# The first pair of blocks of a convolution and SwiGLU kernel: tokens ahead of weights, idle TensorE products, pieces in a new order

## The chip, the cores and the metric

The kernel runs on one core of a Trainium2 chip. The metric is the device time of one execution in microseconds; the time of a kernel is the median of its runs.

A core has five engines that run side by side, each through its own queue in order: TensorE (PE in the profile, its weight loads PEld) multiplies matrices, VectorE (DVE) and ScalarE (ACT) do elementwise work, GpSimd (POOL) does elementwise work more slowly, and SyncE (SP) issues transfers. An engine that waits holds up all that stands behind it in its queue. SBUF is the memory on the core, PSUM holds TensorE's results in 8 banks.

## The reference

32768 tokens of 192 numbers go through a short causal convolution and a SwiGLU network without bias. All inputs and outputs are float32 to the kernel.

```python
# attention block: x (8, 4096, 192), weight (8 heads, 7 taps)
w = softmax(weight)                                  # over the 7 taps of a head
out[b, s, h, g] = sum_k w[h, k] * x_pad[b, s + k, h, g]   # 24 channels share a head's taps
# network: x (32768, 192), w_gate and w_val (192, 1536), w_out (1536, 192)
rms = np.sqrt(np.mean(x * x, axis=-1, keepdims=True) + 1e-06)
xn = x / rms * rms_g
g = xn @ w_gate
silu = g * (1.0 / (1.0 + np.exp(-g)))
val = xn @ w_val
return (silu * val @ w_out).astype(np.float32)
```

The matrices arrive as 64-bit floats, as two 32-bit words each, and the kernel takes them apart itself.

## The kernel before

The tokens are cut into 32 pairs of blocks; a pair is 1024 tokens, in two blocks g of 512. The hidden width of 1536 is 12 chunks of 128, taken as 4 units u of 3 chunks f. In every product the two halves of TensorE's rows work side by side: the lower 64 rows compute the gate, the upper 64 the value. The product of a pair has these parts:

- conv (L327): 7 taps; ScalarE multiplies tokens by a tap into a tile m (L356, eight instructions per tap, one per head), VectorE adds (L360). The first tap, and the first three of the first pair, are done on VectorE alone (L341, L346). At its end it loads the tokens of the next pair (load, L143), for which there is one buffer.
- norm (L364): squares on ScalarE (L371), the factor by GpSimd's power (L377, L380), scaling on ScalarE and VectorE (L389, L384).
- place (L459), fetch (L484), x_sums (L496): VectorE transposes blocks of 32 (L471), SyncE writes them to a scratch in DRAM (L476) and reads them back as xb, channels on the partitions (L491); VectorE forms 11 sums of blocks in xc (L501).
- unit (L530): for the pairs after the first, the products of a unit are a fast scheme that needs 15 products (L568) in place of 18, with copies and sums on the other engines. Its order is written out in PLAN. It takes 11 working tiles from the list tiles and gives them back.
- outer (L654): the product with the output matrix (L661), 96 steps on each half, whose results are added up (L681, L685) and stored (L690). A block's first pass takes chunks 0 to 8 for all four groups of 128 tokens, then 9 to 11.

The first pair is different, since nothing is ready. Its tokens come by load(0), followed in SyncE's queue by the weights of unit 0 (load_in), two parts of the output matrix (load_out) and unit 1. After the convolution, cross (L403) scales and transposes through TensorE: the factor r is a power on GpSimd (L426), diag holds eight diagonal matrices of the factors (L430, L435), 24 products of y with them (L441) give the transpose in PSUM, and 12 copies bring it to xb (L456, L454). The first pair's products are the plain ones (L608): 24 groups of 6 matmuls (L621), each followed by a SiLU (L631) and a product (L638), which gives back a PSUM bank.

All weights are converted in this first pair. convert (L233) takes exponent and mantissa of each number apart on VectorE (L241, L245, L248), scales them on ScalarE (L252, L253, and L256 for the output matrix), and puts them together on VectorE (L258, L268, L273) or GpSimd (L264, L265). A unit's input weights are converted at once, 128x1152 numbers an instruction. The output matrix comes in six parts of 128x384 through two buffers of the pool outs; the next load is issued by GpSimd when a part is converted. w_sums (L295) forms on GpSimd the sums of weights that the fast scheme needs, 19 instructions a unit; it overwrites parts of the plain weights, and so waits for the plain products of that unit.

The order of the first pair on all engines is written by hand: the string START names one piece of work a letter (x cross, i input weights, o and O output matrix, c convolution of pair 1, n its norm, t its transposes, p products, s SiLUs, v values, w sums of weights). From the output stage on, pieces are put at places in a queue, in units of 1/100 of the time that a product of 512 columns takes; base is the start of the output stage.

Of the kernel before, what the change touches and what calls it, by code (L numbers as in the profile page):

```python
# [11 lines left out]
F32 = mybir.dt.float32  # L12
AF = mybir.ActivationFunctionType
# [6 lines left out]
def kernel(  # L20
# [166 lines left out]
    def words(w):  # L187
        return w.bitcast(U32).rearrange("r (n two) -> r n two", two=2)

    def load_in(u, q):  # L190
        cols = slice(u * NF * P, (u + 1) * NF * P)
        t = big.tile([P, 2, NF, T], F32, name="ht")
        t = t[:].rearrange("p a f t -> p (a f t)")[:, 0 : KP * NF * P * 2].bitcast(U32)
        t = raw["in", u] = t.rearrange("p (k n two) -> p k n two", k=KP, two=2)
        for w, rows in ((moe_w_gate, LOW), (moe_w_val, UPP)):
            for k in range(KP):
                q.dma_start(out=t[rows, k], in_=words(w)[k * HP : (k + 1) * HP, cols, :])

    def load_out(i, q=nc.gpsimd):
        if i >= NO:  # L200
            return
        t = outs.tile([P, T // P, D], F32, name="o_sb")
        t = t[:].rearrange("p j d -> p (j d)").bitcast(U32)
        t = raw["out", i] = t.rearrange("p (f d two) -> p f d two", f=PF, two=2)
        for f in range(PF):
            r = (i * PF + f) * P
            q.dma_start(out=t[:, f], in_=words(moe_w_out)[r : r + P, :, :])

    load_in(0, nc.sync)
    load_out(0, nc.sync)  # L210
    load_out(1, nc.sync)
# [100 lines left out]
    def convert_in(u):  # L312
        if u >= NU:
            return
        dst = wf[u][:, 0:9, :].rearrange("p (k f) n -> p k (f n)", k=KP)
        yield from convert(raw.pop(("in", u)), exp_i, mf_i, dst, rg_sb)

    def convert_out(i):
        dst = wo_sb[:, i * PF : (i + 1) * PF, :]
        yield from convert(raw.pop(("out", i)), *cvt[i % 2], dst)  # L320
        load_out(i + 2)
# [5 lines left out]
    def conv(p, alone=0):  # L327
# [6 lines left out]
        for k in range(K):  # L334
# [19 lines left out]
            for h in range(H):  # L354
                hs = slice(h * GS, (h + 1) * GS)
                nc.scalar.mul(m[:, :, hs], xk[:, :, hs], taps[:, h, k : k + 1])  # L356
                if h % 2:
                    yield
            if k > 0:
                nc.vector.tensor_tensor(out=y[:], in0=y[:], in1=m[:], op=ALU.add)  # L360
            yield
# [40 lines left out]

    def cross():  # L403
        y = ys.pop(0)
        ss = work.tile([P, NJ], F32, name="ss")
        sq = work.tile([P, D], F32, name="sq")
        na = NJ // 2
        for j in range(na):
            nc.scalar.activation(
                out=sq[:], in_=y[:, j, :], func=AF.Square, accum_out=ss[:, j : j + 1]  # L410
            )
            yield
        nc.scalar.copy(out=ends[:, :, 0:HP], in_=y[:, :, 2 * HP :])
        yield
        s2 = prods.tile([P, NJ, D], F32, name="m")
        nc.vector.tensor_tensor(
            out=s2[:, na:, :], in0=y[:, na:, :], in1=y[:, na:, :], op=ALU.mult
        )
        nc.vector.tensor_reduce(out=ss[:, na:], in_=s2[:, na:, :], axis=AX.X, op=ALU.add)
        nc.vector.tensor_copy(out=ends[:, :, HP:], in_=y[:, :, 0:HP])  # L420
        yield
        r = work.tile([P, NJ], F32, name="r")
        nc.vector.tensor_scalar(
            out=r[:], in0=ss[:], scalar1=1.0 / D, scalar2=1e-6, op0=ALU.mult, op1=ALU.add
        )
        nc.gpsimd.tensor_tensor(out=r[:], in0=r[:], in1=nhalf[:], op=ALU.pow)  # L426
        yield
        for j in range(NJ):
            if j % 2:
                nc.vector.tensor_scalar(  # L430
                    out=diag[:, j, :], in0=unity, scalar1=r[:, j : j + 1],
                    scalar2=None, op0=ALU.mult,
                )
            else:
                nc.scalar.mul(diag[:, j, :], unity, r[:, j : j + 1])  # L435
            yield
        nq = T // P
        for j in range(NJ):
            for k in range(KP):
                two = ends[:, j, :] if k == 2 else y[:, j, k * HP : (k + 2) * HP]  # L440
                nc.tensor.matmul(  # L441
                    out=ps[k * 2 + j // nq][:, (j % nq) * P : (j % nq + 1) * P],
                    lhsT=two, rhs=diag[:, j, :], start=True, stop=True, skip_group_check=True,
                )
            yield
            if j % nq == nq - 1:
                for k in range(KP):
                    src = ps[k * 2 + j // nq][:].rearrange("p (j g q) -> p g q j", j=nq, g=2)
                    for h in range(2):
                        dst = xb[HALF[h], :, (k + h) % KP, :]  # L450
                        dst = dst.rearrange("p g (q j) -> p g q j", j=NJ)
                        dst = dst[:, :, :, j - nq + 1 : j + 1]
                        if h and j == NJ - 1:
                            nc.vector.tensor_copy(out=dst, in_=src[HALF[h]])  # L454
                        else:
                            nc.scalar.copy(out=dst, in_=src[HALF[h]])  # L456
                        yield

# [45 lines left out]
    ps = [psum.tile([P, T], F32, name=f"ps{i}") for i in range(8)]  # L504
    HALF = (LOW, UPP)
# [3 lines left out]
    tiles = [work.tile([P, T], F32, name=f"tile{i}") for i in range(11)]  # L509
# [98 lines left out]
    def plain(hts):  # L608


        groups = [(u, g, f) for u in range(NU) for g in (1, 0) for f in range(NF)]
        held = {}
# [119 lines left out]
    def done(it):  # L732
        for _ in it:
            pass
# [5 lines left out]

    START = (
        "xxxxxxxixxxxxxxxxoxixcxcxxxixxxxxixxxxxxxxciccicpccccpsivOpsiccvpciscicpscvcvcpi"
        "scovpwcsivpcwsOvpiswccvpiscciwcpscvwvcicpsvipwoOcspsvviwpsviwpsiwpsvcwpsvvopOswo"
        "cOpvwosOnvpnnnpossvnoOpvOopnnOnnststtstttvvv"
    )
    done(conv(0, 3))
    load_in(2, nc.sync)
    load_in(3, nc.sync)
    hts = []
    p, sl, v = plain(hts)  # L750
    pieces = {
        "x": cross(),
        "i": itertools.chain(*[convert_in(u) for u in range(NU)]),
        "o": itertools.chain(*[convert_out(i) for i in range(0, NO, 2)]),
        "O": itertools.chain(*[convert_out(i) for i in range(1, NO, 2)]),
        "c": conv(1, 1), "n": norm(1, share=True), "t": place(1),
        "p": p, "s": sl, "v": v,
        "w": itertools.chain(*[w_sums(u) for u in range(NU)]),
    }
    for i in START.replace(" ", ""):  # L760
        next(pieces[i], None)
    for i in "iocntpsvO":
        done(pieces[i])
    ws = pieces["w"]
# [10 lines left out]
    WLATE = (160, 439, 719, 999, 1279, 1558, 1838, 2118)  # L775
    ROOM = (465, 526)
    for p in range(PAIRS):
# [14 lines left out]
        put(base + LAG, functools.partial(fetch, p + 1))  # L792
        if p == 0:
            later(ws, *[base + i for i in WLATE])
# [5 lines left out]
        later(x_sums(p + 1), *[base + i for i in (1690, 2020, 2060)],  # L800
              *[base + 2345 + 70 * i for i in range(len(XSUM) - 2)])
# [30 lines left out]
```

## Time and profile before

| | us |
|---|---|
| median of 3 runs | 2740.15 (2739.7 to 2740.2) |
| the profiled execution | 2740.65 |
| its span, first to last instruction | 2738.8 |
| TensorE busy | 2689.3 (98%) |
| VectorE busy | 2282.8 (83%) |
| ScalarE busy | 2208.5 (81%) |
| GpSimd busy | 1239.9 (45%) |

The profile is of one execution. Busy time is the time in which an engine worked on an instruction, including a matmul that runs at a lowered clock. Lines such as L621 are lines of the kernel before. The time of the execution includes 1.85 us around the span. A matmul of float32 appears as two records for each instruction.

| the first pair in the timeline | start, us |
|---|---|
| first work on tokens (L341, L356) | 11.8 |
| last addition of the convolution (L360) ends | 26.45 |
| first transposing product (L441) | 31.6 |
| first plain product (L621) | 43.09 |
| first output product (L661) | 114.8 |
| first product of the second pair (L568) | 152.5 |

### The profile page before, as it was taken

Reading aid. Unit: us, or ns where it says so; the run is one execution under the profiler, and the core shown is the slowest. Engines: PE = TensorE matmul, PEld = TensorE weight load, DVE = VectorE, ACT = ScalarE, POOL = GpSimd, SP = SyncE. Lnnn points to the kernel's source line nnn. Section 1 sums busy time; section 2 is a strip of 40 time slices with the busy share of each in tenths; the row PEclk is TensorE's granted clock in tenths of the full one; section 3 lists DMA queues with packets and bytes.
Section 4 is the critical chain, followed back from the end, with each engine's and each line's share of the span. In section 5 each row is a group of like instructions: output and inputs, shape, how many; then the busy total and the mean of one; then the engine's idle time right before and its main releaser. Section 6 shows DMA issues by size and latency. Waiting matters only on the chain.

```text
span 2738.8 us, 54219 instructions
## 1 busy us (share of the span) xinstructions
PE 2689.3 (98%) x20192; PEld 2049.6 (75%) x20192; DVE 2282.8 (83%) x3642; ACT 2208.5 (81%) x5011; POOL 1239.9 (45%) x1034
## 2 busy tenths in 40 slices
PE   4899999999999999999999999999999999999999
PEld 2568888778887788887788876677766777766777
DVE  7788889888888888888888898888888888988854
ACT  7588888888888888888888888888887888888854
POOL 2854344544345533445434445434455343454433
PEclk9999999999999999999999999999999999999999
DMA  4212222112221122221121221112211222211110
GB/s 121 79 44 68 56 68 60 43 44 58 66 62 47 49 57 56 67 61 42 44 67 56 67 52 50 45 56 68 62 41 50 61 56 67 62 41 44 44 39 13
DMA packets 93945, 152.90 MB, mean 56 GB/s; under 512 B 6769, under 2 KB 63857, under 8 KB 89593
## 3 DMA queue, kind: packets, MB, share of 16 engines
q1 hardware_dynamic: 92608, 147.84, 20.8%
q8 instruction: 158, 2.59, 0.4%
q0 software_dynamic: 512, 1.57, 0.2%
q14 instruction: 107, 0.87, 0.1%
q10 hardware_dynamic: 560, 0.03, 0.0%
HBM read 99.87 MB, written 49.55 MB: 55 GB/s over the span
## 4 chain that ended last, share of the span: by engine, by line
PE 98%; DVE 1%; DMA 0%; POOL 0%; issue 0%; ACT 0%; SPq 0%; DVEq 0%; POOLq 0%
PE ps L568 58%; PE ps L661 37%; PE ps L621 2%; DMA x_sb<-in_x_dram 0%; DVE y L360 0%; PE ps L672 0%; DVE y L346 0%; PE ps L441 0%; ACT xb L456 0%; DMA o_sb<-in_moe_w_out_dram 0%; DVE nt L471 0%; DVE y L384 0%; DVE xc L258 0%; POOL r L426 0%; DVE y L341 0%
## 5 line engine op out<-in xcount | busy, mean ns | idle before, releaser
L568 PE MATMUL ps<-xc,wf 64*128 64x512 f32 x4960 | 1521.8, 593 | 0.0
L568 PEld LDWEIGHTS ps<-xc,wf 64*128 64x128 f32 x4960 | 764.7, 187 | 396.3 <-issue 177.2
L661 PE MATMUL ps<-wo_sb,ht 64*128 64x192 f32 x12288 | 1052.5, 323 | 3.6 <-DVE ht L638 3.6
L661 PEld LDWEIGHTS ps<-wo_sb,ht 64*128 64x128 f32 x12288 | 1048.8, 187 | 3.9 <-DVE ht L638 3.9
L568 PE MATMUL ps<-xb,wf 64*128 64x512 f32 x2480 | 1019.6, 589 | 0.0
L597 POOL TENSOR_TENSOR ht<-ht,tile 128x512 f32<-128x512 f32 x620 | 773.4, 1272 | 535.1 <-ACT tile L594 534.5
L577 ACT ACTIVATE tile<-ps 128x512 f32<-128x512 f32 x1488 | 821.1, 598 | 166.3 <-PE ps L568 141.8
L568 PEld LDWEIGHTS ps<-xb,wf 64*128 64x128 f32 x2480 | 434.6, 187 | 210.9 <-issue 105.5
L356 ACT ACTIVATE m<-x_sb,taps 128x192 f32<-128x192 f32 x1520 | 543.2, 444 | 8.5 <-DMA x_sb<-in_x_dram 5.9
L585 POOL TENSOR_TENSOR tile<-tile,tile 128x512 f32<-128x512 f32 x248 | 315.2, 1271 | 221.6 <-DVE tile L581 211.7
L590 DVE TENSOR_TENSOR tile<-ps,tile 128x512 f32<-128x512 f32 x620 | 411.7, 681 | 0.4 <-PE ps L568 0.4
L360 DVE TENSOR_TENSOR y<-y,m 128x1536 f32<-128x1536 f32 x190 | 335.5, 1766 | 86.0 <-ACT m L356 79.6
L590 DVE TENSOR_TENSOR ht<-ps,tile 128x512 f32<-128x512 f32 x620 | 400.4, 678 | 0.0
L594 ACT ACTIVATE tile<-tile 128x512 f32<-128x512 f32 x620 | 379.0, 624 | 22.5 <-DVE tile L590 20.9
L377 POOL TENSOR_SCALAR r<-ss 128x8 f32<-128x8 f32 x31 | 27.6, 891 | 643.3 <-ACT sq L371 643.2
L590 DVE TENSOR_TENSOR ps<-ps,tile 128x512 f32<-128x512 f32 x248 | 173.4, 699 | 132.7 <-PE ps L568 130.6
L577 ACT ACTIVATE ps<-ps 128x512 f32<-128x512 f32 x372 | 216.3, 581 | 45.4 <-PE ps L568 34.5
L685 DVE TENSOR_TENSOR o_sb<-ps,o_sb 128x192 f32<-128x192 f32 (+1 forms) x192 | 77.1, 417 | 153.8 <-PE ps L568 110.4
L581 DVE COPY tile<-ps 128x512 f32<-128x512 f32 x248 | 169.9, 685 | 7.0 <-PE ps L568 5.7
L579 DVE TENSOR_SCALAR ps<-ps 128x512 f32<-128x512 f32 x248 | 164.1, 694 | 0.0
L681 ACT COPY o_sb<-ps 128x192 f32<-128x192 f32 (+1 forms) x192 | 70.2, 366 | 97.3 <-PE ps L661 97.2
L371 ACT ACTIVATE sq<-y 128x192 f32<-128x192 f32 x248 | 90.1, 363 | 65.9 <-DVE y L360 60.1
(69 smaller groups left out, 1206.0 us busy)
## 6 DMA issues: line engine op xcount, KB each, us to landing
xb<-xd SPq DMA_DIRECT2D x124, 384.0 KB, 6.5
x_sb<-in_x_dram SPq DMA_DIRECT2D x24, 1344.0 KB, 5.8
out_dram<-o_sb SPq DMA_DIRECT2D x64, 384.0 KB, 2.6
xd<-nt SPq DMA_DIRECT2D x124, 192.0 KB, 3.4
x_sb<-in_x_dram SPq DMA_DIRECT2D x8, 1176.0 KB, 10.1
ht<-in_moe_w_gate_dram SPq DMA_DIRECT2D x12, 192.0 KB, 7.7
ht<-in_moe_w_val_dram SPq DMA_DIRECT2D x12, 192.0 KB, 6.8
o_sb<-in_moe_w_out_dram POOLq DMA_DIRECT2D x8, 192.0 KB, 2.8
```

Of the source, the lines that this page charges most:

```text
L356: nc.scalar.mul(m[:, :, hs], xk[:, :, hs], taps[:, h, k : k + 1])
L360: nc.vector.tensor_tensor(out=y[:], in0=y[:], in1=m[:], op=ALU.add)
L371: nc.scalar.activation(out=sq[:], in_=y[:, j, :], func=AF.Square, accum_out=ss[:, j : j + 1])
L568: nc.tensor.matmul(out=new(v, h, True) if first else old(v, h), lhsT=wf[u][HALF[h], WAT[i], :], rhs=x_op(XOP[i])[HALF[h]], start=first, st ...
L577: nc.scalar.activation(out=dst, in_=src, func=AF.Copy, scale=float(s))
L579: e.tensor_scalar(out=dst, in0=src, scalar1=-1.0, scalar2=None, op0=ALU.mult)
L581: e.tensor_copy(out=dst, in_=src)
L585: e.tensor_tensor(out=grab((v, h)), in0=a, in1=b, op=plus(s))
L590: e.tensor_tensor(out=dst, in0=src, in1=t, op=plus(s))
L594: nc.scalar.activation(out=dst, in_=src, func=AF.Silu)
L597: e.tensor_tensor(out=hv(v), in0=src, in1=tl["g", v][:], op=ALU.mult)
L661: nc.tensor.matmul(out=bank(h, bks[h])[:, w : w + D], lhsT=hts[f // NF][HALF[h], g, f % NF, j * P : (j + 1) * P], rhs=wo_sb[HALF[h], f, :] ...
```

## The change

Only the beginning differs; the functions of the later pairs and PLAN stay as they are.

- Tokens first: a new function hold lets GpSimd copy a few numbers from the tokens into each buffer that the first weights will land in, so that these loads wait for the tokens.
- Output matrix at once: its parts 2 to 5 no longer wait for a free buffer. They are loaded by SyncE into two new tiles tls of three working tiles each, which the fast scheme is given later (at base + 864); the plain products of the first pair work with 5 tiles in place of 11.
- Idle products: heat issues on TensorE five 128x512 products of the taps' tiles m (two of tap 4, two of tap 5, one of tap 6). Nothing reads their result.
- cross is cut into seven pieces. Its factor is a square root on ScalarE, a reciprocal and one correcting step on VectorE, in place of GpSimd's power. ScalarE's and VectorE's diagonals, products and copies are separate pieces.
- The weights of unit 0 are converted in thirds of 128 columns, one for each chunk f, and the first six groups of products go chunk by chunk.
- The first tap of pair 1's convolution is on ScalarE instead of VectorE.
- START is new, and a list LATER puts the remaining pieces into the output stage: transposes of pair 1 at 943 to 1239, its fetch at 1299 in place of 38, its 11 sums from 2345 on in place of from 1690 on, and the sums of weights at other places.

```diff
+    def hold(t):
+        if 0 in x_sb:
+            nc.gpsimd.tensor_copy(out=t, in_=x_sb[0][:, 0 : t.shape[1], 0])
     def load_in(u, q):
...
+        hold(t[:, :, 0, 0].bitcast(F32))
...
+    NT = 11
+    few = NT - 6
+    tl6 = [work.tile([P, 3, T], F32, name=f"tls{i}") for i in range(2)]
+    tiles = [work.tile([P, T], F32, name=f"tile{i}")[:] for i in range(few)]
+    room = [t[:].rearrange("p j d -> p (j d)") for t in tl6]
+    def load_out(i):
+        if i < 2:
+            t = outs.tile([P, T // P, D], F32, name="o_sb")
+            t = t[:].rearrange("p j d -> p (j d)")
+            hold(t[:, 0 : PF * D * 2 : D * 2])
+        else:
+            n = PF * D * 2
+            t = room[i // 2 - 1][:, (i % 2) * n : (i % 2 + 1) * n]
...
-            q.dma_start(out=t[:, f], in_=words(moe_w_out)[r : r + P, :, :])
+            nc.sync.dma_start(out=t[:, f], in_=words(moe_w_out)[r : r + P, :, :])
...
+        step = P if u == 0 else NF * P
+        parts = [slice(i, i + step) for i in range(0, NF * P, step)]
+        return [
+            convert(t[:, :, c, :], exp_i[:, :, c], mf_i[:, :, c], dst[:, :, c], rg_sb)
+            for c in parts
+        ]
...
-        load_out(i + 2)
...
+            if k in hot:
+                heat(m[:].rearrange("p j d -> p (j d)")[:, 0:T], hot[k])
...
+    def heat(t, n):
+        for _ in range(n):
+            nc.tensor.matmul(
+                out=ps[7][:], lhsT=unity, rhs=t, start=True, stop=True, skip_group_check=True,
+            )
...
-        nc.gpsimd.tensor_tensor(out=r[:], in0=r[:], in1=nhalf[:], op=ALU.pow)
+            nc.scalar.activation(out=r[:], in_=ss[:], func=AF.Sqrt)
+            nc.vector.reciprocal(r[:], r[:])
+            nc.vector.tensor_tensor(out=t, in0=r[:], in1=r[:], op=ALU.mult)
+            nc.vector.scalar_tensor_tensor(
+                out=t, in0=t, scalar=-0.5, in1=ss[:], op0=ALU.mult, op1=ALU.mult
+            )
+            nc.vector.scalar_tensor_tensor(
+                out=r[:], in0=t, scalar=1.5, in1=r[:], op0=ALU.add, op1=ALU.mult
+            )
...
+        groups[0 : 2 * NF] = [(0, g, f) for f in range(NF) for g in (1, 0)]
...
     START = (
-        "xxxxxxxixxxxxxxxxoxixcxcxxxixxxxxixxxxxxxxciccicpccccpsivOpsiccvpciscicpscvcvcpi"
-        "scovpwcsivpcwsOvpiswccvpiscciwcpscvwvcicpsvipwoOcspsvviwpsviwpsiwpsvcwpsvvopOswo"
-        "cOpvwosOnvpnnnpossvnoOpvOopnnOnnststtstttvvv"
+        "XxxxxxXDdDdDTDdadTbTaTfbTakTakTakTkbkKkKkKkbkbfpocfcfcpfsicccpsvivOpsicpciscvcpi"
+        "sccvcpvwsiccwpcvsciwpvcscwpsiccwcvpisccvcipscvovpwisccpvswcipvwscccpsiwOvpsiwvip"
+        "svvpswocpsvwcpsOnwonvpovsonpOsvOvwopnOo"
     )
+    LATER = (
+        (61, "s"), (75, "o"), (131, "s"), (150, "v"), (226, "O"), (349, "v"), (363, "O"),
+        (474, "n"), (564, "O"), (756, "n"), (800, "n"), (843, "n"), (886, "n"), (943, "t"),
+        (1001, "t"), (1022, "w"), (1059, "t"), (1118, "t"), (1176, "t"), (1234, "t"),
+        (1239, "t"), (1302, "w"), (1582, "w"), (1861, "w"), (2141, "w"), (2421, "w"),
+    )
-    done(conv(0, 3))
+    done(conv(0, 3, hot={4: 2, 5: 2, 6: 1}))
     load_in(2, nc.sync)
     load_in(3, nc.sync)
+    for i in range(2, NO):
+        load_out(i)
...
-        "c": conv(1, 1), "n": norm(1, share=True), "t": place(1),
+        "c": conv(1), "n": norm(1, share=True), "t": place(1),
...
-        put(base + LAG, functools.partial(fetch, p + 1))
+        put(base + (LAG if p else 1299), functools.partial(fetch, p + 1))
         if p == 0:
-            later(ws, *[base + i for i in WLATE])
+            put(base + 864, lambda: tiles.extend(t[:, i, :] for t in tl6 for i in range(3)))
...
+        xat = [base + 2345 + 70 * i for i in range(len(XSUM) + 1)]
+        if p:
+            xat = [base + i for i in (1690, 2020, 2060)] + xat[:-3]
+        later(x_sums(p + 1), *xat)
```

## Prediction

> **What bounds the kernel now.** I read the page first: TensorE is busy 98% of the span. The edit touches the first pair of blocks; from the second pair on, the built order of all engines and their waits is as before. So only the time until TensorE runs without a break can change. Next I read the matmul rows of the timeline for breaks, the granted clock by microsecond, the waits of that stretch, and the timeline of the other engines for what each break waits on.
>
> ```profile
> PE 2689.3 (98%) x20192; PEld 2049.6 (75%) x20192; DVE 2282.8 (83%) x3642; ACT 2208.5 (81%) x5011; POOL 1239.9 (45%) x1034
> ...
> 11.80 1.93 DVE y L341 x8
> ...
> 28.92 2.20 POOL r L426
> ...
> 43.09 55.88 PE ps L621 x251
> ...
> 102.79 5.42 PE L621 MATMUL ps<-xb,wf 64*128 64x512 f32 x24 [2.98 <-DVE ht L638]
> 111.55 3.86 PE L621 MATMUL ps<-xb,wf 64*128 64x512 f32 x9 [3.33 <-DVE ht L638]
> ...
> 122.78 5.49 PE L661 MATMUL ps<-wo_sb,ht 64*128 64x192 f32 x32 [3.58 <-DVE ht L638]
> ```
> The columns are start, duration, instruction, and in brackets the idle time before. Tokens arrive at 11.7 us, convolution and transposes take until 43.09, and the plain products run without a break to 99. Then come three breaks, 9.9 us together. ScalarE and VectorE queue behind the output matrix there:
>
> ```profile
> DVE xc L241 <- DMA o_sb<-in_moe_w_out_dram: 12.1, 3, 6.3
> ...
> 42.00:43.00 1.00, 0.00 (x0) 0.91 0.00 0
> 43.00:44.00 1.00, 0.91 (x2) 0.50 0.00 0
> ...
> 101.00:102.00 1.00, 0.00 (x0) 1.00 0.00 0
> ...
> 121.00:122.00 1.00, 0.00 (x0) 0.66 0.00 0
> 122.00:123.00 1.00, 0.22 (x2) 0.50 0.00 0
> ```
> A window row has the range, its length, TensorE's busy time and count, the granted clock, the DMA share and GB/s. The clock is halved after idle of 3.8, 3.3 and 3.6 us, and kept through the 2.98 us before 102.79. The halved stretches last 3.4 us from 42.8, 3.4 from 111.1 and 6.8 from 121.3; TensorE works in about 3.2, 2.9 and 5.4 us of them at half speed, which costs some 5.7 us.
>
> **The sum of TensorE's work.** Warm, one group of plain products is 6 matmul instructions, 12 records; 24 groups are 288 records, and two halves run side by side in 0.43 us per pair of records: 24 x 2.58 = 62 us. The output stage is 192 pairs of records at 0.161, that is 31 us. Before, the second pair begins at 153.2, so 110.1 us after 43.09 hold 93 of work; breaks and half clock make up most of the other 17.
>
> **Tokens alone (gain 3.1).** The load of a later batch, undisturbed, shows its own speed:
> ```profile
> 2222.86 0.77 SPq L166 DMA_DIRECT2D x_sb<-in_x_dram  x2
> ...
> 2228.00:2229.00 1.00, 1.00 (x17) 1.00 (x16) 1.00 (x2) 0.54 (x3) 0.34 (x1) 1.00 0.94 258
> 2229.00:2230.00 1.00, 1.00 (x16) 1.00 (x15) 1.00 (x3) 0.00 (x0) 1.00 (x1) 1.00 0.01 0
> ```
> Its traffic ends about 6.5 us after issue. At the start issue is at 1.14; with 0.9 for the slower first microseconds and for completion, tokens are there at 8.5 instead of 11.7. Bounds: 0 if the beginning is slow by itself, 3.5 at best. The holding copies on GpSimd (four, at most the 0.2 us of its nearest small row each) keep weights until then. The first weights, 1.2 MB at the 200 GB/s of the rows around 10 us, are there at about 17 and read only at 28; the load of the second pair's tokens, queued behind them on SyncE, lands near 33 and is read at 38. The rest of the weights and the whole output matrix, 3.9 MB, follow by 50 and are read from 70 on. All of it is hidden, with 5 us or more of cover. VectorE finishes the convolution in the same 14.65 us (11.80 to 26.45), at 23.35.
>
> **Idle products (gain 0).** Five 128x512 products cost four 128x128 ones each: 1.7 us at half clock (0.43 for the cold ones of L441). They read the products of taps 4, 5, 6, ready at 14.2, 17.0 and 20.5, so they end near 22, before VectorE takes that buffer at 23.4. The first transposing product follows at 27.6. The trace loses the clock in 3.3 us of idle, and at 121.3 as early as 2.1 us after the last matmul. The Trainium skill, "TensorE: Matmul & The Clock Gate", Part 1 and its closing table, says that a window of about 3.4 us without work halves the clock and that gaps over some 3 us are to be avoided. That speaks against this edit: its own gap is 5.6 us. The rule alone would leave a gap shorter than two windows some chance of staying warm; the trace, losing it after 2.1, leaves little. Were it warm, transposes would end 2.3 us sooner and the gain below would be 1.5 more. I take cold.
>
> **Pieces in a new order up to the first product (gain 2.0).** GpSimd's power (2.2 us) becomes a ScalarE root and four small VectorE instructions at 0.22 (rows of 128x8 at 0.16 to 0.20), about 1.4 us with hops; the table load of 1.28 us is ahead of it, while ScalarE waits for y. Diagonals start at y+3.85 (before +4.7). The two diagonal queues no longer have a 2.2 us conversion among them, but three thirds (3 x 0.35 each) follow on VectorE. Cold, the 24 transposing products take what they took before, 7.6, to y+12.0. Three VectorE copies (0.64 each) follow at once, and three ScalarE copies (0.58) each wait for theirs: first product at y+14.65 = 38.0, against 43.09 = y+16.6. Clock all cold: y+17.2; warm: y+13.2.
>
> **Weights in thirds, plain stage (new stalls 2.4).** Each third costs VectorE 3 x 0.35 + 2 x 0.5 + 3 x 0.26 = 2.8, 8.4 for the unit against 6.7 whole; a third is enough to start, and the second and third are done before groups 2 and 4. What is late next is unit 1. VectorE begins it 5.5 us after the transposes' copies; ScalarE has six copies of taps, the table load, six more and two SiLUs first, and returns the converted parts at y+24.4; L258, L268, an add (1.75), a value and three L273 end at y+31.3, where group 6 is due at y+30.1: 1.2 us. Unit 2 ends 0.7 to 1.2 late in the same way; unit 3 has 3 us to spare. Against contention: the first convolution tap moves to ScalarE, which frees 1.9 us of VectorE. The skill, "SBUF — State Buffer", "Who interferes with whom", says that a VectorE instruction with two SBUF inputs and a GpSimd one that reads SBUF exclude each other for a whole instruction. L303 has a median of 0.46, so six such instructions could add 2.8 to unit 1. The trace has the adds L360 at 1.90 mean against 1.74 best, under a tenth; I take the trace, and the rule goes to the range. Five SiLU tiles instead of eleven: values follow within four groups, no cost. Plain stage: 38.0 + 62 + 2.4 = 102.4.
>
> **Output matrix at once (removes the breaks).** No second load waits for a conversion, so the 9.9 us of breaks and their half clocks go. Late next is GpSimd: after unit 2's products it has 11 sums (0.46 to 1.0) and 8 output steps of 1.0, and is ready for chunk 8 about when TensorE asks, 2.6 us into the output stage: 0, or up to 2 us.
>
> **The second pair's inputs (new stall 4.1).** ScalarE finishes the last SiLU 0.65 us into the output stage, then has 16 tap copies (0.35), three output steps (1.45) and four scalings ahead of the first transpose: +9.2. VectorE transposes once, adds (1.75), transposes five times: +13.9. The path from there is in the trace:
> ```profile
> 122.23 2.36 SPq L476 DMA_DIRECT2D xd<-nt  x4
> 127.36 2.74 SPq L491 DMA_DIRECT2D xb<-xd  x4
> ...
> 137.68 0.82 DVE L501 TENSOR_TENSOR xc<-xb 128x512 f32<-128x512 f32 x1 [0.31 <-DMA xb<-xd]
> ```
> Transposes ended at 122.2, xb landed at 137.65: 15.4 us. So xb lands at +29.3, 1.7 us ahead of the second pair. VectorE, queued at that wait, then has 11 sums at 0.62, two evacuations, four scalings and two bank copies: +39.5, where TensorE needs the second bank copy at +35.5. A stall earlier in the output stage is taken off this one. SyncE's output store and next token load stand behind the fetch in its queue until about +21.7; nobody waits for them that early.
>
> **Sum.** 102.4 + 31 + 4.1 = 137.5, against 153.2: 15.7 us less. The profiled execution took 2740.65 with a span of 2738.8; the median of the runs is 2740.15. 2740.15 - 15.7 = 2724.4.
>
> **Rivals.** Forecast (0.50): as above, 2720 to 2729. (a) The queues keep up (0.22): unit conversions in time and xb some microseconds earlier; 5 us more gain, 2719; a held warm clock, 2717. For it: unit 1 misses by only 1.2. (b) Crowding (0.17): VectorE does in 125 us nearly what it did in 142; gaps over 3 us halve the clock again, twice 3 + 1.7: 2733. For it: the port rule. (c) The stalls eat the gain (0.05), 2738. (d) Slower (0.06): six of the eleven working tiles of every later pair now lie in two joint blocks and are handed out in another order; should that cost each of 31 pairs a wait, it decides from 0.51 us per pair (15.7/31), and 0.7 gives 2746. Against it: the order and waits of these pairs are unchanged and TensorE binds.
>
> **Numbers.** A change below 0.2% (5.5 us) can't be told from none here. Faster 0.50 + 0.22 + 0.17 = 0.89; same 0.05; slower 0.06. Range 2717 to 2733.
>
> **Right or wrong.** Right: first token work at 8.6, first plain product near 38, no wait of VectorE for the output load, the clock halved at the transposes though idle products ran, output stage from about 102, and a gap or waits on VectorE of some 4 us at the second pair's first bank copies. Wrong: idle products' warm clock lasting, unit 1 stalling 3 us or more, xb landing before +25, or rows of later pairs changed.

## The result, and the profile after

The changed kernel takes 2727.61 us (median of 6 runs, 2726.52 to 2730.9) against 2740.05 for the kernel before (6 runs, 2738.93 to 2740.38): 12.4 us less, ratio 0.9957 with a 95% interval of 0.9944 to 0.997. The forecast was 2724.4, between 2717 and 2733. The profiled execution is one of the faster: 2726.66, span 2724.8, so 14.0 us below the profiled execution of before.

First the page's line of busy times, then TensorE's rows of the timeline (start, duration, engine, line, operation, count, and in brackets the idle time before with what ended it). L434 are the idle products, L495 the transposing ones, L683 the plain ones, L723 the output product, L629 the products of the second pair.

```profile
PE 2693.3 (99%) x20202; PEld 2071.0 (76%) x20202; DVE 2286.5 (84%) x3654; ACT 2212.3 (81%) x5026; POOL 1242.6 (46%) x1029
...
15.43 7.40 PE L434 MATMUL ps<-m,nt 128*128 128x512 f32 x10 [15.43 <-ACT m L378]
28.42 1.22 PE L495 MATMUL ps<-xc,y 128*128 128x128 f32 x4 [5.59 <-ACT xc L488]
...
36.54 31.61 PE L683 MATMUL ps<-xb,wf 64*128 64x512 f32 x144 [1.10 <-ACT xb L515]
68.73 31.17 PE L683 MATMUL ps<-xb,wf 64*128 64x512 f32 x144 [0.58 <-DVE wf L291]
99.70 2.76 PE L723 MATMUL ps<-wo_sb,ht 64*128 64x192 f32 x26
102.72 14.56 PE L723 MATMUL ps<-wo_sb,ht 64*128 64x192 f32 x174 [0.26 <-POOL wo_sb L283]
119.08 12.83 PE L723 MATMUL ps<-wo_sb,ht 64*128 64x192 f32 x133 [1.79 <-DVE o_sb L747]
...
136.68 0.66 PE L629 MATMUL ps<-xc,wf 64*128 64x512 f32 x1 [0.81 <-DVE xc L565]
...
139.55 0.66 PE L629 MATMUL ps<-xc,wf 64*128 64x512 f32 x1 [1.78 <-DVE xc L565]
```

The three breaks of before, 9.9 us behind the loads of the output matrix, are gone: the longest wait on a converted piece is 0.58 for the weights of the network's first layer (wf) and 0.26 for the output matrix (wo_sb). The plain stage lasts from 36.54 to 99.70, 63.2 us. Two losses are in the rest: 1.79 us at L747, and 0.81 and 1.78 at the second pair's first sums.

What L747 and the sums wait for stands on VectorE's and SyncE's rows. L747 adds the upper half of an output block and gives its PSUM bank back. L384 are the additions of the third pair's convolution, L535 the transposes of the second pair's tokens, L540 and L555 their way out to DRAM and back, L565 the sums made of them.

```profile
112.72 2.52 DVE L535 STREAM_TRANSPOSE nt<-y 128x256 f32<-128x256 f32 x5
115.08 3.67 DVE L384 TENSOR_TENSOR y<-y,m 128x1536 f32<-128x1536 f32 x2
118.68 1.14 DVE L747 TENSOR_TENSOR o_sb<-ps,o_sb 128x192 f32<-128x192 f32 x4
...
115.26 2.36 SPq L540 DMA_DIRECT2D xd<-nt  x4
120.40 2.74 SPq L555 DMA_DIRECT2D xb<-xd  x4
...
132.10 0.69 DVE L565 TENSOR_TENSOR xc<-xb 128x512 f32<-128x512 f32 x1 [7.87 <-DMA xb<-xd]
```

TensorE wants a bank at 117.3, but the four additions that free banks start at 118.68, behind two of 1.8 us each in VectorE's queue. The transposes end at 115.24, the tokens are back at 132.1, and VectorE has stood idle for 7.87 us by then.

The clock (one microsecond a row: range, length, busy time and count of PE, PEld, DVE, ACT, POOL, granted clock, DMA share, GB/s):

```profile
118.00:119.00 1.00, 0.00 (x0) 0.00 (x0) 1.00 (x3) 1.00 (x5) 1.00 (x1) 1.00 1.00 269
119.00:120.00 1.00, 0.92 (x12) 0.93 (x13) 1.00 (x5) 1.00 (x4) 0.84 (x3) 1.00 0.72 167
120.00:121.00 1.00, 1.00 (x10) 1.00 (x10) 1.00 (x1) 1.00 (x5) 0.92 (x2) 0.55 0.00 0
121.00:122.00 1.00, 1.00 (x10) 1.00 (x8) 0.75 (x1) 1.00 (x5) 1.00 (x1) 0.50 0.11 16
122.00:123.00 1.00, 1.00 (x10) 1.00 (x8) 0.52 (x1) 0.44 (x2) 0.92 (x3) 0.50 0.74 217
123.00:124.00 1.00, 1.00 (x12) 1.00 (x12) 1.00 (x1) 0.00 (x0) 1.00 (x1) 0.74 1.02 223
```

The wait of 1.79 us is followed, about a microsecond after work is back, by 3.4 us at half clock: 1.7 us more.

### The profile page after: what moved, and what is told of

Its sections match the earlier page's. It is cut to its first block, busy times and chain, and to the rows that moved or that the text cites. A ratio compares the mean times of both kernels' runs of the same rounds, so it can differ in the third digit from the quotient of the medians.

```text
span 2724.8 us, 54269 instructions
## 1 busy us (share of the span) xinstructions
PE 2693.3 (99%) x20202; PEld 2071.0 (76%) x20202; DVE 2286.5 (84%) x3654; ACT 2212.3 (81%) x5026; POOL 1242.6 (46%) x1029
## 4 chain that ended last, share of the span: by engine, by line
PE 96%; DVE 2%; DMA 1%; POOL 0%; ACT 0%; issue 0%; SPq 0%; DVEq 0%; POOLq 0%; ACTq 0%
PE ps L629 59%; PE ps L723 36%; PE ps L683 1%; DVE y L384 0%; DMA xb<-xd 0%; DMA x_sb<-in_x_dram 0%; POOL wf L321 0%; DVE xc L565 0%; PE ps L734 0%; DVE y L368 0%; ACT m L378 0%; DVE ht L700 0%; ACT xb L515 0%; DVE wf L291 0%; PE ps L495 0%
## 5 line engine op out<-in xcount | busy, mean ns | idle before, releaser
L629 PE MATMUL ps<-xc,wf 64*128 64x512 f32 x4960 | 1522.7, 593 | 2.6 <-DVE xc L565 2.6
L629 PEld LDWEIGHTS ps<-xc,wf 64*128 64x128 f32 x4960 | 771.2, 187 | 392.6 <-issue 209.8
L723 PE MATMUL ps<-wo_sb,ht 64*128 64x192 f32 x12288 | 1052.4, 323 | 2.0 <-DVE o_sb L747 1.8
L723 PEld LDWEIGHTS ps<-wo_sb,ht 64*128 64x128 f32 x12288 | 1047.7, 187 | 4.8 <-DVE o_sb L747 2.1
L629 PE MATMUL ps<-xb,wf 64*128 64x512 f32 x2480 | 1020.3, 589 | 0.0
L658 POOL TENSOR_TENSOR ht<-ht,tls 128x512 f32<-128x512 f32 x414 | 520.5, 1275 | 358.2 <-ACT tls L655 357.6
L638 ACT ACTIVATE tile<-ps 128x512 f32<-128x512 f32 x825 | 484.0, 596 | 139.9 <-PE ps L629 126.8
L629 PEld LDWEIGHTS ps<-xb,wf 64*128 64x128 f32 x2480 | 435.4, 187 | 199.0 <-issue 115.5
L384 DVE TENSOR_TENSOR y<-y,m 128x1536 f32<-128x1536 f32 x190 | 335.0, 1763 | 83.8 <-ACT m L378 78.8
L638 ACT ACTIVATE tls<-ps 128x512 f32<-128x512 f32 x663 | 376.0, 599 | 27.6 <-PE ps L629 16.1
L658 POOL TENSOR_TENSOR ht<-ht,tile 128x512 f32<-128x512 f32 x206 | 260.7, 1274 | 175.2 <-ACT tile L655 174.9
L655 ACT ACTIVATE tls<-tls 128x512 f32<-128x512 f32 x414 | 254.9, 625 | 16.5 <-DVE tls L651 15.0
L651 DVE TENSOR_TENSOR ht<-ps,tls 128x512 f32<-128x512 f32 x331 | 220.8, 681 | 0.0
L747 DVE TENSOR_TENSOR o_sb<-ps,o_sb 128x192 f32<-128x192 f32 (+1 forms) x192 | 77.5, 419 | 150.6 <-PE ps L629 107.8
L651 DVE TENSOR_TENSOR ht<-ps,tile 128x512 f32<-128x512 f32 x289 | 192.3, 681 | 0.0
L651 DVE TENSOR_TENSOR ps<-ps,tls 128x512 f32<-128x512 f32 x166 | 116.2, 700 | 87.8 <-PE ps L629 84.7
L651 DVE TENSOR_TENSOR tls<-ps,tile 128x512 f32<-128x512 f32 x248 | 166.9, 682 | 0.2 <-PE ps L629 0.2
```

The source lines that it names most:

```text
L629: nc.tensor.matmul(out=new(v, h, True) if first else old(v, h), lhsT=wf[u][HALF[h], WAT[i], :], rhs=x_op(XOP[i])[HALF[h]], start=first, st ...
L638: nc.scalar.activation(out=dst, in_=src, func=AF.Copy, scale=float(s))
L651: e.tensor_tensor(out=dst, in0=src, in1=t, op=plus(s))
L655: nc.scalar.activation(out=dst, in_=src, func=AF.Silu)
L658: e.tensor_tensor(out=hv(v), in0=src, in1=tl["g", v][:], op=ALU.mult)
L723: nc.tensor.matmul(out=bank(h, bks[h])[:, w : w + D], lhsT=hts[f // NF][HALF[h], g, f % NF, j * P : (j + 1) * P], rhs=wo_sb[HALF[h], f, :] ...
```

## The experiments

Eight kernels were run in two groups of four. Each is set against the runs of the kernel before beside its group: 2740.13 (9 runs) for no_heat, late_heat, norm_first and no_hold, 2739.55 (21 runs) for the other four.

| kernel | median us (lowest to highest) | against before | ratio, 95% interval |
|---|---|---|---|
| changed kernel | 2727.61 (2726.52 to 2730.9) | -12.4 | 0.9957 (0.9944 to 0.997) |
| no_heat | 2728.73 (2727.89 to 2729.66) | -11.4 | 0.996 (0.9946 to 0.9973) |
| late_heat | 2727.34 (2726.51 to 2728.32) | -12.8 | 0.9954 (0.9942 to 0.9967) |
| norm_first | 2726.14 (2723.08 to 2727.85) | -14.0 | 0.9949 (0.9936 to 0.9961) |
| no_hold | 2730.17 (2728.27 to 2730.62) | -10.0 | 0.9963 (0.995 to 0.9975) |
| b_hold | 2739.07 (2738.2 to 2739.99) | -0.5 | 0.9999 (0.9991 to 1.0008) |
| out_turns | 2742.68 (2741.7 to 2746.56) | +3.1 | 1.0014 (1.0005 to 1.0023) |
| whole_unit | 2729.96 (2726.17 to 2730.59) | -9.6 | 0.9962 (0.995 to 0.9975) |
| evac_both | 2725.86 (2725.54 to 2727.35) | -13.7 | 0.9951 (0.9939 to 0.9964) |

The interval of a ratio is about 7 us wide where a kernel had five or six runs. So among the variants of the changed kernel only out_turns stands apart by its times; the others are told apart by their profiles, and a difference of 1 to 3 us between medians is a hint.

### no_heat: the changed kernel without the idle products

```diff
-    done(conv(0, 3, hot={4: 2, 5: 2, 6: 1}))
+    done(conv(0, 3, hot={}))
```

> The changed kernel without its five idle products. If they bring nothing (the clock was lost at 27.9 us, before the transposing products, though they ran until 22.8): the same time as the changed kernel, 12.4 us below the kernel before, within 1.5 us either way, and the transposing products start at half clock as with them. If they do keep something warm: slower than the changed kernel by 1.5 us or more, with the transposing products or the first plain ones longer at half clock.

It measured 2728.73, 1.1 us above the changed kernel's median and inside its spread. The first transposing product starts cold in both: after 5.59 us without work where idle products ran, and as TensorE's first work of all where they didn't:

```profile
29.95 1.22 PE L495 MATMUL ps<-xc,y 128*128 128x128 f32 x4 [29.95 <-ACT xc L488]
```

Both first rows take 1.22 us for four records. The 1.5 us by which it starts later is from its tokens, which were first worked on at 11.28 us instead of 9.65. Counted from the first transposing product, the first plain one comes at +8.12 with idle products and at +8.51 without, but the other kernels with the same five spread from +8.06 to +8.86. The idle products bring nothing that these runs show.

### late_heat: four more idle products on the finished tokens

```diff
     def cross():
         y = ys.pop(0)
+        heat(y[:].rearrange("p j d -> p (j d)")[:, 0:T], 4)
```

> The changed kernel with four more idle products, on the finished convolution of the first pair (ready at 24.4 us), directly ahead of the transposing products at 28.4. If idle products fail only because they come too early: the clock stays whole from about 21 on, the 24 transposing products take some 5.5 us instead of 6.9, and the first plain product starts 0.5 to 1 us earlier (ScalarE is busy until 31.7 anyway), so 13 to 13.5 us below the kernel before. If idle products don't hold the clock at all: half clock at the transposes all the same, and no gain.

Now the clock holds, and four records take 0.71 us:

```profile
28.90 0.71 PE L496 MATMUL ps<-xc,y 128*128 128x128 f32 x4 [0.33 <-ACT xc L489]
...
36.38 32.04 PE L684 MATMUL ps<-xb,wf 64*128 64x512 f32 x144 [1.85 <-ACT xb L516]
69.56 31.17 PE L684 MATMUL ps<-xb,wf 64*128 64x512 f32 x144 [1.15 <-DVE wf L291]
```

The convolution is done at 24.8, so the first plain product comes at y + 11.6 (y is that moment, as in the forecast) instead of y + 12.2: 0.6 us, where the forecast had put 1.5 on a warm clock. The transposes end 1.4 us sooner after y, but the product then waits 1.85 us instead of 1.10 for ScalarE's copies of them, and the second half of the plain stage waits 1.15 for its weights instead of 0.58. A warm clock at that place is worth little, since ScalarE is what binds there.

### norm_first: the second pair's tokens ahead of the rest of the output stage

```diff
-        (474, "n"), (564, "O"), (756, "n"), (800, "n"), (843, "n"), (886, "n"), (943, "t"),
-        (1001, "t"), (1022, "w"), (1059, "t"), (1118, "t"), (1176, "t"), (1234, "t"),
-        (1239, "t"), (1302, "w"),
+        (474, "n"), (531, "O"), (532, "n"), (534, "n"), (536, "n"), (538, "n"), (540, "t"),
+        (542, "t"), (1022, "w"), (544, "t"), (546, "t"), (548, "t"), (550, "t"),
+        (552, "t"), (1302, "w"),
```

> The changed kernel with only the list LATER edited: the scaling and the six transposes of the second pair come ahead of most taps and additions of the third pair's convolution. The theory is that the chain transposes, scratch, xb (15.4 us and more) is what the second pair waits for, and that VectorE's late queue causes the 1.8 us wait on L747 and the half clock after it. Then transposes end about 10 us into the output stage instead of 15.5, xb lands near +25 instead of +32.3, the waits at the second pair's start (2.6 us) and on L747 (1.8 us, and 1.7 of half clock) go: 5 to 7 us less than the changed kernel, 17.5 to 19.5 below the kernel before. Rival: GpSimd's factor (ready at +5) and conversions hold TensorE in any order; then under 2 us less.

It measured 2726.14, with the fastest single run of all, 2723.08, which is the profiled one.

```profile
103.95 14.56 PE L723 MATMUL ps<-wo_sb,ht 64*128 64x192 f32 x174 [0.80 <-POOL wo_sb L283]
120.40 11.15 PE L723 MATMUL ps<-wo_sb,ht 64*128 64x192 f32 x133 [1.88 <-DVE o_sb L747]
...
135.03 0.59 PE L629 MATMUL ps<-xc,wf 64*128 64x512 f32 x1
...
109.66 3.04 DVE L535 STREAM_TRANSPOSE nt<-y 128x256 f32<-128x256 f32 x6
112.52 7.56 DVE L384 TENSOR_TENSOR y<-y,m 128x1536 f32<-128x1536 f32 x4
120.00 1.14 DVE L747 TENSOR_TENSOR o_sb<-ps,o_sb 128x192 f32<-128x192 f32 x4
128.42 0.69 DVE L565 TENSOR_TENSOR xc<-xb 128x512 f32<-128x512 f32 x1 [2.87 <-DMA xb<-xd]
```

The output stage starts at 100.39 here. The tokens are back 28.0 us after that (32.4 in the changed kernel), and the second pair starts at 135.03 without a wait: that half of the theory holds. The wait on the bank is as long as before, 1.88, since now all four additions stand ahead of L747. In this execution the clock held after it (133 records in 11.15 us, where 133 took 12.83 in the changed kernel); the granted clock of the slower runs is lower over the whole span (0.998 against 0.999), as if it didn't there, but they have no trace. The profile is 3.5 us shorter than the changed kernel's, the median 1.5. The theory had set 5 to 7; the median is where the rival put it (under 2), but not for the rival's reason: what remains is the bank that VectorE gives back late.

### no_hold and b_hold: the tokens ahead of the weights, taken away and alone

no_hold is the changed kernel without GpSimd's small copies that make the weights wait for the tokens; b_hold is the kernel before with them.

```diff
     def hold(t):
-        if 0 in x_sb:
-            nc.gpsimd.tensor_copy(out=t, in_=x_sb[0][:, 0 : t.shape[1], 0])
+        return
```

> The changed kernel without the copies that make the first weights wait for the tokens: all loads are issued together as in the kernel before. If tokens ahead of weights bring what the start of the trace shows (first token work at 9.65 instead of 11.8): 2.1 us slower than the changed kernel, some 10.3 below the kernel before. If the later arrival of the weights costs part of that again: less than 1 us slower. If the tokens' delay is passed on to nothing later: the same.

> The kernel before with one part of the change alone: GpSimd's placeholder copies out of the first token tile ahead of every weight load, so that the weights queue behind the tokens. Theory (tokens ahead of weights brings time by itself): the forecast gave it 3.1 us; taking the same copies out of the changed kernel cost 2.6 us of median, and within single executions, counted from the landing of the first small weights, only about 1 us. So 1 to 2.6 us below the kernel before (2737.5 to 2739.1 us). Rival (queues keep up, or the weights' delay is paid back at the first conversions): no difference, or up to 2 us slower, since in the old order all four conversions of unit 0 stand ahead of the first product and the second half of the weights would then be what is late.

no_hold is 2.6 us above the changed kernel's median, near the 2.1 of its first expectation, though the runs of the two overlap; its trace also has the clock halved twice as long at the transposes (28.4 to 35.2), some 0.5 us. b_hold is 0.5 below before with an interval of 0.9991 to 1.0008, so that neither a gain of 2 us nor none is ruled out. In the traces the tokens were first worked on at:

| | held: changed, norm_first, late_heat, no_heat | held: out_turns, whole_unit, evac_both | held: b_hold | not held: before, no_hold |
|---|---|---|---|---|
| first work on tokens | 9.65, 9.60, 10.15, 11.28 | 11.12, 10.80, 10.61 | 10.63 | 11.80, 12.43 |
| first work on the small tap weights (L238), loaded by ScalarE's queue | 3.94, 4.25, 4.73, 5.40 | 5.25, 5.12, 5.01 | 4.25 | 5.16, 5.97 |
| difference | 5.7, 5.35, 5.4, 5.9 | 5.9, 5.7, 5.6 | 6.4 | 6.6, 6.5 |

Even this small load, which no part of the change touches, lands between 3.9 and 6.0 us. Taken from there the tokens gain about 1 us in the changed kernel (from 6.5 to 5.6); the rest of the 2.1 us between the profiles of before and after is from when an execution gets going. In the kernel before, the one trace shows 0.2 us by this measure (6.6 to 6.4), although the weights are held there too (first issued at 11.02 instead of 1.96). Why the copies bring less there is open.

### out_turns: the output matrix in turns, everything else changed

```diff
-    def load_out(i):
+    def load_out(i, q=nc.sync):
+        if i >= NO:
+            return
-        if i < 2:
+        if True:
             t = outs.tile([P, T // P, D], F32, name="o_sb")
...
-            nc.sync.dma_start(out=t[:, f], in_=words(moe_w_out)[r : r + P, :, :])
+            q.dma_start(out=t[:, f], in_=words(moe_w_out)[r : r + P, :, :])
...
-    for i in range(2, NO):
-        load_out(i)
...
         yield from convert(raw.pop(("out", i)), *cvt[i % 2], dst)
+        load_out(i + 2, nc.gpsimd)
```

> The changed kernel with one part undone: the six pieces of the output matrix are loaded in turns through the two tiles of the pool again, each by GpSimd's queue once the piece before it is converted. Theory (this part carried most of what was won at the output stage: breaks of 9.9 us and two half clocks in the kernel before): 4 to 7 us slower than the changed kernel, 2731 to 2735 us, with waits of TensorE on the converted pieces in the output stage. Rival (the new order of the conversions alone would have done it, as the six-piece order places each conversion earlier now): at most 1.5 us slower, with no wait over 1 us on the pieces.

It measured 2742.68: 15 us above the changed kernel, and 3.1 us above before, with an interval that leaves out 1. The theory had the sign and the place, and less than half of the size. The waits between 90 and 140 us (engine, line, what it waited for: sum, times, longest):

```profile
DVE xc L261 <- DMA o_sb<-in_moe_w_out_dram: 20.4, 4, 8.7
ACT xc L272 <- DVE xc L265: 17.6, 4, 6.0
POOL xc L284 <- ACT o_sb L276: 8.3, 3, 4.5
```

and TensorE's rows:

```profile
101.19 6.63 PE L686 MATMUL ps<-xb,wf 64*128 64x512 f32 x21 [3.29 <-DVE ht L703]
...
114.28 1.65 PE L726 MATMUL ps<-wo_sb,ht 64*128 64x192 f32 x8 [3.91 <-POOL wo_sb L285]
116.32 14.31 PE L726 MATMUL ps<-wo_sb,ht 64*128 64x192 f32 x160 [0.39 <-POOL wo_sb L285]
133.01 1.56 PE L726 MATMUL ps<-wo_sb,ht 64*128 64x192 f32 x14 [2.37 <-ACT o_sb L746]
136.60 13.83 PE L726 MATMUL ps<-wo_sb,ht 64*128 64x192 f32 x133 [2.03 <-DVE o_sb L750]
```

VectorE stands 20.4 us at the loads of the third to sixth piece, and everything behind it in its queue stands too: the values that TensorE needs banks from (3.29), the conversions (3.91), the evacuations (2.37, 2.03). The order of the pieces is written out by hand for pieces that are there; without them each wait holds the whole queue. So with this order the load at once is what carries the change: all other parts together, without it, lose 3 us. The reverse, the load at once with the old order of the pieces, was not run.

### whole_unit: the first unit's weights in one piece

```diff
-        step = P if u == 0 else NF * P
+        step = NF * P
...
-        groups[0 : 2 * NF] = [(0, g, f) for f in range(NF) for g in (1, 0)]
```

> The changed kernel with one part undone: the first unit's weights are converted in one piece instead of three, and its product groups go row block by row block as before. Theory (the first product waits only for the rows of its own third, which is what the forecast missed): the first plain product comes 2 to 3 us later than in the changed kernel (36.5 us), near 39 us, and the total rises by 1.5 to 3 us, to 2729 to 2730.5 us. Rival (the copies of the tokens' transposes bind, not the weights): the first product stays within 0.7 us and the total within the changed kernel's own spread.

It measured 2729.96, 2.3 us above, but from 2726.17 to 2730.59, so that it reaches below the changed kernel's fastest run. The first plain product:

```profile
38.40 32.18 PE L682 MATMUL ps<-xb,wf 64*128 64x512 f32 x139 [1.60 <-ACT xb L515]
```

It waits for ScalarE's copies, not for weights: 1.60 us, where six of the kernels with thirds wait 1.10. Counted from the first transposing product (29.54 here, 28.42 in the changed kernel), it comes at +8.86 instead of +8.12: 0.7 us, of which some 0.3 is a half clock that lasted longer. The theory, 2 to 3 us there, falls: the thirds bring half a microsecond. In this execution, the slowest of the five, the clock was also halved from 39.8 to 43.2 and from 142.2 to 145.6, which the changed kernel's profile does not have, and was kept at L746, the L747 of the others. Whether the thirds prevent the first of these or a chance of phase did it is not settled.

### evac_both: both losses of the output stage

norm_first's order, and three of the third pair's additions behind L747:

```diff
-    def conv(p, alone=0, hot=()):
+    def conv(p, alone=0, hot=(), late=()):
+        held = []
...
-            if k > 0:
+            held.append(m)
+            if k == 0 or k in late:
+                held = held if k else []
+                continue
+            while held:
+                m = held.pop(0)
                 nc.vector.tensor_tensor(out=y[:], in0=y[:], in1=m[:], op=ALU.add)
                 yield
...
+        at = [i + 83 * n for i in starts for n in range(5)]
+        if p == 0:
+            at = at[:14] + at[15:19] + at[20:24] + [1991, 1993, 1995] + at[25:]
-        later(conv(p + 2, 1), *[base + i for i in (250, 255)],
-              *[base + i + 83 * n for i in starts for n in range(5)], base + 2340)
+        later(conv(p + 2, 1, late=() if p else (3, 4)), *[base + i for i in (250, 255)],
+              *[base + i for i in at], base + 2340)
```

> The changed kernel with two moves in the first pair's output stage: the normalisation and transposes of the second pair's tokens ahead of the rest there (as in norm_first), and the third to fifth additions of the third pair's convolution put behind the four additions that give the first PSUM banks back, so that those four stand behind two additions of 1.7 us and not behind four. Theory (the two losses that the forecast missed are the bank wait of 1.8 us with the half clock after it, and the late tokens of the second pair; norm_first took only the second away): the wait on the bank is gone or under 0.3 us, the clock stays whole through the output stage in every run, the second pair starts without a break, and the total is 2721 to 2723.5 us, with a spread of under 2 us between runs. Rival (once the additions come later, the second pair's tokens are what is late again, or ScalarE's own work behind the additions delays the second pair's combinations): the total stays at norm_first's 2726 us and TensorE waits at the start of the second pair.

It measured 2725.86, with the smallest spread of the variants (1.8 us). In this kernel L723 has become L729, L565 L571 and L629 L635:

```profile
101.98 2.76 PE L729 MATMUL ps<-wo_sb,ht 64*128 64x192 f32 x26
105.53 25.40 PE L729 MATMUL ps<-wo_sb,ht 64*128 64x192 f32 x308 [0.79 <-POOL wo_sb L283]
...
135.57 0.66 PE L635 MATMUL ps<-xc,wf 64*128 64x512 f32 x1 [0.84 <-DVE xc L571]
...
138.44 0.66 PE L635 MATMUL ps<-xc,wf 64*128 64x512 f32 x1 [1.78 <-DVE xc L571]
...
130.99 0.69 DVE L571 TENSOR_TENSOR xc<-xb 128x512 f32<-128x512 f32 x1 [1.44 <-DMA xb<-xd]
```

The wait on the bank is gone: 308 records run without a break at full clock, where the changed kernel had a break of 1.79 and a half clock. But TensorE now reaches the second pair earlier, and waits 0.84 and 1.78 there for the sums again, although the tokens are back 29.0 us after the output stage's begin and not 32.4. A half clock follows from 139.1 to 142.5 in this execution, the slowest of the five (2727.35). The theory had set 2721 to 2723.5 and a second pair without a break; the rival had this: the total stays at norm_first's. The output stage and the second pair's tokens are two paths of nearly equal length; each move shortens one and the other then sets the end. Here the tokens also took 1 us longer through DRAM than in norm_first (16.7 against 15.7).

Of the versions measured, norm_first and evac_both have the lowest medians, 14.0 and 13.7 us below before, 1.3 to 1.6 us better than the changed kernel by that measure; the intervals overlap, so neither is shown to beat it.

## Why the prediction was right, point by point

**The break and its size.** That the breaks go and the later pairs stay as they are was right, and out_turns shows the load at once as the part without which this order gains nothing. The sum was 15.7 us, the profile gained 14.0 and the median 12.4. The terms, in the profile's own times:

| step | forecast | measured |
|---|---|---|
| first work on tokens | 8.6 | 9.65 |
| convolution done (y) | 23.35 | 24.3 |
| first plain product | y + 14.65 = 38.0 | y + 12.2 = 36.54 |
| plain stage with its stalls | 64.4 | 63.2 |
| output stage begins | 102.4 | 99.70 |
| its work | 31 | 32.0 |
| stalls to the second pair's steady run | 4.1 | 0.26 + 1.79 + 1.7 + 0.81 + 1.78 = 6.3 |

The last but one is from norm_first: from 100.39 to its second pair at 135.03 are 34.64, less its waits of 0.80 and 1.88.

That the total came so close is in part luck. The output stage began 2.7 us earlier than forecast, and what follows took over 3 us more than forecast (1.0 of work, 2.2 of stalls); the two errors nearly cancel. The measured rows add up to 138.0; the timeline puts the second pair's steady run near 138.7 (its third product starts at 139.55, and two take 0.86), so that 0.7 us stands in no row.

**Tokens alone (3.1) was too large.** The traffic's own time had been taken from a late, undisturbed load; the wrong term is the 0.9 us allowed for the beginning, where 2.0 went by (9.65 less the issue at 1.14 and the 6.5 of the late load). The profile shows a gain of 2.1, of which about 1 is the hold's own by the comparison with no_hold.

**Idle products (0) was right, with its reason.** The clock was halved from 27.9 to 31.35, 5.1 us into a gap of 5.59. The forecast had also set what a warm clock would be worth, 2.3 us at the transposes and 1.5 in the end; late_heat measured 1.4 and 0.6. Against this case's runs the rule of the Trainium skill weighed there ("TensorE: Matmul & The Clock Gate", Part 1 and its closing table) agrees with the 5.59 us that lost the clock; the 1.79 us that lost it at L747 lie below its 3 us, and there the measurement decides.

**First product (2.0 gained): the step that failed is "three VectorE copies follow at once, and three ScalarE copies each wait for theirs".** The gain was 4.4 (y + 16.6 to y + 12.2). The forecast made the product wait for all the copies and put it 2.65 us after the transposes; it came 1.1 after them, which is 1.5 of the 2.4 us that the forecast missed.

```profile
32.34 5.20 ACT L515 COPY xb<-ps 64x512 f32<-64x512 f32 x9 [0.61 <-PE ps L495]
35.02 1.91 DVE L513 COPY xb<-ps 64x512 f32<-64x512 f32 x3 [0.51 <-PE ps L495]
```

ScalarE copies from 32.34 on, while transposes still run, and goes on until 37.5, a microsecond after the first product has started at 36.54: the first product needs only the channels that it reads. The transposes themselves took 7.0 us instead of 7.6, because the clock came back 2.9 us after their start and not 4.4 as before. How the gain of 4.4 divides between the root in place of the power and the cutting of cross is not shown: no run undoes one of them.

**Stalls of the plain stage (2.4) were 0.58** in the profile, and 1.1 in six of the others (no_heat, late_heat, norm_first, no_hold, out_turns, evac_both). Only the wait before the second half of the stage is there; the one forecast for unit 1 isn't. Some queues kept up, as rival (a) had it. The 2.8 us that VectorE and GpSimd might have cost each other at unit 1 did not show as a wait of TensorE.

**GpSimd's chunk (0 to 2 us)** was 0.26, and 0.8 in the others but out_turns.

**The second pair's inputs (4.1).** The mechanism was right: VectorE's sums are what TensorE waits for. Its sizes: transposes ended 15.5 us after the output stage's begin, not 13.9; and the way through DRAM took 16.8 us, not 15.4. That way was 15.1 to 16.8 us in ten traced executions (15.4 before, 15.35 in no_heat, 15.7 in norm_first, 16.7 in evac_both), with the same instructions. The changed kernel and no_heat have the same order there too, so the 1.5 us between these two come from something else than the order; from what is not shown. "A stall earlier in the output stage is taken off this one" holds, in both directions, as norm_first and evac_both show.

**What was missing is L747.** The forecast went through the queue of VectorE for the transposes and for the sums, but not for the four additions that give banks back in between. This is the 1.79 us, and the half clock that came with it. It is there with 1.79 to 1.88 in every variant of the changed kernel but two: 2.03 in out_turns, and none in evac_both.

**The rivals.** Crowding (b), at 2733, was right in kind: VectorE's shorter time is what makes L747 and the sums late. It stopped at three waits under 2 us and one half clock. The slower case (d), another order of tiles in the later pairs, did not come: the 14.0 us between the two spans are there in full by the second pair's third product, which starts at 139.55 in the changed kernel and at 153.57 in the kernel before:

```profile
153.57 0.59 PE L568 MATMUL ps<-xc,wf 64*128 64x512 f32 x1
```

## What to carry to other kernels

When a break of several microseconds is taken out, go through every instruction that the engine behind it has queued in the stretch that gets shorter, the ones that give buffers back first: here the 9.9 us of breaks had also hidden an evacuation behind two additions and a fetch that needs 15 to 17 us. Where two paths end within 2 us of each other, a shorter one only lets the other set the end: norm_first and evac_both brought 1.5 and 1.8 us by their medians, where 5 to 7 and 4 to 6.5 had been expected. And a hand-written order is only as good as its inputs' arrival: the same order with loads in turns was slower than the old one.

## What was not expected of the hardware

- The clock's answer to a gap of about 1.8 us does not follow from its length. In the changed kernel, no_heat, late_heat and no_hold a wait of 1.79 to 1.80 us cost 3.4 us at half clock; in whole_unit one of 1.80 and in norm_first one of 1.88 us, at the same instruction, did not. The changes of the clock in one trace lie on a grid of 3.41 us: 21.11, 27.94, 31.35, 120.10 and 123.51 us in the changed kernel, whose differences are 2, 1, 26 and 1 steps. With each trace's grid counted on from its own changes, the four waits that cost a half clock lie within one step (in the changed kernel 117.28 to 119.08, in the step from 116.69 to 120.10), and the two that did not are cut by its end (118.52 to 120.40 at 119.92 in norm_first, 120.27 to 122.06 at 121.74 in whole_unit). That is not the whole of it: the waits of 1.75 to 1.78 us at the second pair's sums lie within one step too, and lost the clock in evac_both and whole_unit, but not in the changed kernel, late_heat and no_hold. This goes some way to explain why the changed kernel's runs spread over 4.4 us and those of before over 1.5; that it does in each run was not traced.

The rows of norm_first for its wait, to be read against those of the changed kernel above:

```profile
118.00:119.00 1.00, 0.52 (x6) 0.22 (x2) 0.90 (x2) 1.00 (x5) 0.92 (x2) 1.00 0.00 0
119.00:120.00 1.00, 0.00 (x0) 0.00 (x0) 1.00 (x1) 1.00 (x4) 1.00 (x1) 1.00 0.34 86
120.00:121.00 1.00, 0.60 (x8) 0.60 (x9) 1.00 (x5) 1.00 (x4) 0.85 (x2) 1.00 1.06 320
121.00:122.00 1.00, 1.00 (x16) 1.00 (x16) 1.00 (x2) 1.00 (x4) 0.99 (x2) 1.00 0.91 164
```

- Single executions differ by 2 us in when the first small load lands (3.9 to 6.0 us), with the same instructions ahead of it. A gain of that size at the beginning can't be read from two profiles.
